# Clustered attention and mixture of experts: the sum of values as one more column of the values' products

## The chip, the cores and the metric

The kernel runs on one core of one Trainium2 chip. The metric is the device time of one execution in microseconds (us), from the start of the program on the core to its end. The core has five engines that work through queues of their own: PE (TensorE, matrix products; PEld is its loading of weights), DVE (VectorE), ACT (ScalarE), POOL (GpSimd) and SP (SyncE, which issues the transfers). Each queue is worked off in order, so an instruction that waits holds up all that stand behind it on its engine.

## The reference

An attention over clusters feeds a mixture of eight experts. Shortened:

```
q, k, v: (B=4, H=8, S=768, D=64); centroids: (8, 16, 64)
mask   = cluster(q)[..., :, None] == cluster(k)[..., None, :]     # cluster: argmax over 16 centroids
scores = where(mask, q @ k.T / 8, -1e9);  scores -= scores.max(-1)
attn   = exp(scores);  attn /= attn.sum(-1) + 1e-9
x      = attn @ v                                                # to (3072, 512)
P      = exp(x @ w_gate - max), then 8 rounds of normalizing over experts and over rows
out    = sum over e of P[:, e] * (relu(x @ w1[e]) @ w2[e])       # w1: (8, 512, 1024), w2: (8, 1024, 512)
```

A query whose cluster holds no key of its head has only masked scores. They are all equal, so its row is the mean of the head's values. This is the case of a "query without a key" that the change is about.

## The kernel before, in words

The program has two stages. The first is the attention, at 0 to about 490 us; the second is the experts, from about 487 us on, with a short overlap.

**Attention.** The 32 heads (4 batches of 8) are worked as 16 pairs. For one pair the 768 queries are cut into 512 and 256 columns and the 768 keys into six tiles of 128; CHUNKS holds nine pieces for each head, of which six are one key tile by 512 queries and three are two key tiles by 256 queries. For each head the stages are these:

- `max_chunk` (L845, L849): products for the row maxima, and a reduction on DVE.
- `max_rows` (from L857): the six maxima of a query become one, split into two half-precision rows that the scores' product subtracts. It also writes `flags` (L871), one where a query has no key, and makes `mz` (L894, ACT), the same mark as a row, which two transfers for each head put into `nht` (L908).
- `exp_chunk` (L926, L927, L933, L955): the scores' products, the exponential on ACT into a tile `pe`, and the sum of `pe` over key tiles, on POOL for all but the last pair, where DVE may do it. There are PB = 14 tiles `pe`.
- `values` (L991, L999): for one pair `av` collects `vn` (values, stationary) by `pe` (moving) over the six key tiles, in three blocks of eight products; each f32 product shows as two instructions. Two more products, `ve` by `nht` (L999), add the mean of the values where a query has no key. ACT then copies `av` to `xT` (L1011).
- `norm` (L1029 to L1113): the sums over keys, with 1e-9 and `flags` added (L1045), their reciprocal, spread over a tile `bc` by transfers, and the product with `xT` (L1086; for the last pair L1113).

`load_group` loads the values of four heads and makes their mean. For the first two of the eight groups it does so by twelve products with ones (L599), for the other six by two reductions on DVE (L607) and one product of two instructions (L611). Three small steps (L614, L618, L622) write it to `ve`. The pair's values can start once this is done.

**Experts.** Every product of the experts runs on PE in an order written out by hand (`run_pe`: L1600 and L1784); DVE, ACT and POOL prepare inputs and weights and gather outputs around it. The inputs of a batch are brought to a common scale by a power of two. For batches 0 to 2 this scale is found during the attention. For batch 3 `next_x` does it among the experts' products: it loads the batch (`xqB`), takes the largest value for each partition on DVE (L330, four reductions, and L1508), and finds the largest over partitions with `powers_spread`: a transfer to memory (L281), a transfer back that spreads all values to each partition (L284), a reduction on DVE (L288) and a few small steps (L290 to L313). Then ACT scales the inputs (L1516), they are split (L1526, L1528), stored (L1531) and loaded as `x6` (L1562).

There is a second way to the same scale, `powers` (L258): a PE transpose (L262), a reduction on DVE (L264), three small DVE steps (L266 to L269) and a small PE product (L272) that spreads the result. It is used in the attention.

**Order.** A planner writes the order of all instructions ahead of time. Each step names its engine, a planned duration and what it waits for; each has an urgency (KEYS); the planner then simulates the engines and fixes each engine's queue. Tokens stand for buffers (`t_pe` for `pe`, `t_x` for PSUM tiles, `t_nh` for `nht`). On the chip the order of each queue stays as planned, whatever the real durations are.

Of the kernel before, what the change touches and what calls it, by code (L numbers as in the profile page):

```python
# [8 lines left out]
F32 = mybir.dt.float32  # L9
# [15 lines left out]
P = 128  # L25
# [154 lines left out]
def attn_moe_kernel(  # L180
# [24 lines left out]
    PB = 14  # L205
# [17 lines left out]
    row = const.tile([2, 1], F32, name="row")  # L223
    nc.gpsimd.iota(row, pattern=[[0, 1]], base=0, channel_multiplier=1, allow_small_or_imprecise_dtypes=True)
    sgn = const.tile([2, 1], F32, name="sgn")
    nc.vector.tensor_scalar(out=sgn, in0=row, scalar1=-2.0, scalar2=1.0, op0=ALU.mult, op1=ALU.add)
    first = const.tile([2, 1], F32, name="first")
    nc.vector.tensor_scalar(out=first, in0=row, scalar1=-1.0, scalar2=1.0, op0=ALU.mult, op1=ALU.add)

# [127 lines left out]
    with ExitStack() as actx:  # L357
# [88 lines left out]
        flags = [sm.tile([P, 2 * NT], F32, name=f"flags{i}", bufs=1) for i in range(4)]  # L446
        row4 = sm.tile([4, 1], F32, name="row4", bufs=1)
        nc.gpsimd.iota(row4, pattern=[[0, 1]], base=0, channel_multiplier=1, allow_small_or_imprecise_dtypes=True)
        up2 = sm.tile([4, 1], F32, name="up2", bufs=1)
        nc.vector.tensor_scalar(out=up2, in0=row4, scalar1=2.0, scalar2=None, op0=ALU.is_ge)  # L450
        odd = sm.tile([4, 1], F32, name="odd", bufs=1)
        nc.vector.scalar_tensor_tensor(out=odd, in0=up2, scalar=-2.0, in1=row4, op0=ALU.mult, op1=ALU.add)
        sgn4 = sm.tile([4, 1], F32, name="sgn4", bufs=1)
        nc.vector.tensor_scalar(out=sgn4, in0=odd, scalar1=-2.0, scalar2=1.0, op0=ALU.mult, op1=ALU.add)
        halves = sm.tile([4, G, D], F32, name="halves", bufs=1)
        for x in range(2):
            c_ = sm.tile([4, 1], F32, name=f"of{x}", bufs=1)
            nc.vector.tensor_scalar(out=c_, in0=up2, scalar1=float(x), scalar2=1.0 / S, op0=ALU.is_equal, op1=ALU.mult)
            for g in range(x, G, 2):
                nc.vector.tensor_copy(halves[:, g], c_.broadcast_to([4, D]))  # L460
# [14 lines left out]
        minus = const.tile([P, 1], F32, name="minus")  # L475
        nc.vector.memset(minus, -1.0)
# [77 lines left out]
        t_nat, t_sc, t_pe, t_nh, t_vn = Tokens(2), Tokens(1), Tokens(PB), Tokens(6), Tokens(2)  # L554
        t_half = Tokens(2)
        t_sum = Tokens(4)
        t_mean, t_norm, t_row = Tokens(1), Tokens(2), Tokens(1)
# [18 lines left out]
        def load_group(n):  # L576
            b, g = n // H, n % H // G
            hs = slice(g * G, (g + 1) * G)
            if True:
                yield ev["x", 0, 1, "k"]  # L580
            if n >= G:
                yield ev["e", 0]
            yield t_vn
            t = groups[(b, g)] = {}
            yield SP, 0.625
            vn = vals.tile([P, G, NT, D], F32, name="vn")
            nc.sync.dma_start(
                out=vn.rearrange("p h t d -> p h (t d)"), in_=v[b, hs].rearrange("h (p t) d -> p h (t d)", t=NT)
            )
            yield plan.copied(3.2) - plan.now.time  # L590

            plan.now.key = urgency("vsum", n)
            yield t_mean
            if n < 2 * G:
                yield t_x
                yield PE, 1.3, 0.107, 0.12
                ps = misc_tile()
                for i in range(NT):
                    nc.tensor.matmul(ps[:, 0 : G * D], ones, vn[:, :, i, :], start=(i == 0), stop=(i == NT - 1))  # L599
            else:  # L600
                vsum = None
                for i in range(2):
                    yield DVE, 1.5
                    if i == 0:
                        vsum = nat.tile([P, G, D], F32, name="vsum", bufs=1)
                    hh = slice(i * G // 2, (i + 1) * G // 2)
                    nc.vector.tensor_reduce(out=vsum[:, hh], in_=vn[:, hh].rearrange("p h t d -> p h d t"), axis=AX, op=ALU.add)  # L607
                yield t_x
                yield PE, 0.64, 0.107, 0.213
                ps = misc_tile()  # L610
                nc.tensor.matmul(ps[:, 0 : G * D], ones, vsum.rearrange("p h d -> p (h d)"), start=True, stop=True)  # L611
            yield DVE, 0.4
            ms = sm.tile([4, G * D], F32, name="ms", bufs=1)
            nc.vector.tensor_tensor(out=ms, in0=ps[0:4, 0 : G * D], in1=halves.rearrange("p h d -> p (h d)"), op=ALU.mult)  # L614
            t_x.put(plan)
            yield ACT, 0.45
            mh = sm.tile([4, G * D], F32R, name="mh", bufs=1)
            nc.scalar.activation(mh, ms, AF.Copy, scale=sgn4)  # L618
            yield ev["cleared"]
            yield "DVE*", 0.4  # L620
            ve = ves[n // G % 2]
            nc.vector.scalar_tensor_tensor(  # L622
                out=ve[0:4].rearrange("p h d -> p (h d)"), in0=ms, scalar=odd, in1=mh.bitcast(F32), op0=ALU.mult, op1=ALU.add
            )
            t_mean.put(plan)
            t.update(vn=vn, ve=ve)
            ev["group", b, g].set(plan)
# [227 lines left out]
        def max_rows(n):  # L855
# [4 lines left out]
            if n >= 8:  # L860
                yield ev["norm", n // 2 - 4]
            yield t_x
            yield DVE, 0.6
# [3 lines left out]
            o = n % 2 * NT  # L867
# [3 lines left out]
            nc.vector.tensor_scalar(out=flags[n // 2 % 4][:, o : o + NT], in0=mr, scalar1=-BIG / 2, scalar2=None, op0=ALU.is_le)  # L871
            ev["flags", n].set(plan)
            half = ps.bitcast(F16)
            if n < 2:
# [5 lines left out]
                nc.tensor.transpose(out=half[0 : 2 * NT, P : 2 * P], in_=two.rearrange("p j t -> p (j t)"), identity=ident_h)  # L880
# [11 lines left out]
            yield ACT, 0.3  # L892
            mz = sm.tile([NT, P], F32R, name="mz")
            nc.scalar.activation(mz, half[0:NT, P : 2 * P], AF.Relu, scale=-4.0 * MARK / BIG, bias=minus[0:NT, :])  # L894
            t_x.put(plan)
            if n >= 2:
# [6 lines left out]
            yield t_nh  # L903
            yield ev["cleared"]
            yield SP, 1.25
            nh = nhs[n // 2 % 3]
            for j in range(n % 2 * 2, n % 2 * 2 + 2):
                nc.sync.dma_start(out=nh[j : j + 1, :].bitcast(F32).rearrange("o (t p) -> o t p", p=P), in_=mz.bitcast(F32))  # L908
            ev["nh", n].set(plan, plan.copied(0.2))

        def exp_chunk(n, c):
# [47 lines left out]
        def release(p, c):  # L959

            c2 = c + 1 if c == 0 else c
            for x in range(2):
                yield ev["s", 2 * p + x, c2]
                t_pe.put(plan)

        def values(p):
# [10 lines left out]
            ve = gr["ve"][:, h % G : h % G + 2].rearrange("p h d -> p (h d)")  # L977
            nh = nhs[p % 3]
            av = None
            for u in range(NCH // VU):  # L980
# [14 lines left out]
            for x in range(2):  # L995
                yield ev["nh", n + x]
            yield PE, 0.44, 0.107, 0.11
            for a, z in SPANS:
                nc.tensor.matmul(av[:, a:z], ve, nh[:, a:z], start=False, stop=True, skip_group_check=True)  # L999
            if h % G == G - 2:  # L1000
                t_vn.put(plan)
            for x in range(2):
                t_nh.put(plan)
                ev["v", n + x].set(plan)
            if h == 0:
                if b:
                    yield ev["batch", b - 1]
                xts[b] = sm.tile([P, NC, S], F32, name="xT", bufs=1)
            for a, z in SPANS:
                yield ACT, 0.15 + (z - a) * 0.00083  # L1010
                nc.scalar.copy(xts[b][:, h // 2, a:z], av[:, a:z])  # L1011
# [5 lines left out]
        def norm(p):  # L1017
# [23 lines left out]
            for x in range(2):  # L1041
                yield ev["flags", n + x]
            yield DVE, 0.2
            rs = work.tile([P, R], F32, name="rs")
            nc.vector.scalar_tensor_tensor(  # L1045
                out=rs.rearrange("p (g j) -> p g j", g=4),
                in0=ps2[:, 0 : NT // 2 * P].rearrange("p (j g q) -> p g j q", g=4, q=Q)[:, :, :, 0],
                scalar=1e-9,
                in1=flags[p % 4].rearrange("p (g j) -> p g j", g=4),
                op0=ALU.add,  # L1050
                op1=ALU.add,
# [5 lines left out]
            if p < npairs - 1:  # L1057
# [24 lines left out]
                x_ = xts[b][:, h // 2, :]  # L1082
# [828 lines left out]
```

## Time and profile before

| | |
|---|---|
| time, median of 3 runs | 2285.37 us (2284.19 to 2285.90) |
| time of the profiled execution | 2290.8 us |
| its span, first to last instruction | 2289.0 us |
| PE busy | 2207.9 us, 96% |
| DVE busy | 1877.2 us, 82% |
| ACT busy | 1201.2 us, 52% |
| POOL busy | 1375.3 us, 60% |
| mean granted TensorE clock | 0.989 |

The profiled execution is one run of its own, 5.4 us above the median; 1.8 us of it lie outside the span. Busy shares are averages over both stages. The stage of the experts takes about 1,800 us, so that the shares of the page are mostly its shares.

### The profile page before, as it was taken

The page shows a single profiled execution, that of the slowest core. Times are in us where ns is not written, and L with a number is a line of the kernel's source. Part 1 is how long each engine was busy: PE and PEld are TensorE (multiplying, and loading weights), DVE is VectorE, ACT ScalarE, POOL GpSimd, SP SyncE. Part 2 cuts the span into 40 slices and gives each one's busy share as a digit, 9 for nine tenths or more (in the row PEclk, how much of TensorE's full clock was granted, in tenths as well). Part 3 has the DMA queues.
Part 4 walks back from the last instruction along what each step waited for, and adds up shares of the span by engine and source line. Part 5 has one row for each costly group of instructions (what it writes and reads, how often), then busy time and mean ns, then how long its engine had stood idle before and what let it go on. Part 6 is the DMA issues. An engine that isn't in the chain of part 4 may idle for free.

```text
span 2289.0 us, 43195 instructions
## 1 busy us (share of the span) xinstructions
PE 2207.9 (96%) x16246; PEld 1530.3 (67%) x16246; DVE 1877.2 (82%) x3684; ACT 1201.2 (52%) x2325; POOL 1375.3 (60%) x1328
## 2 busy tenths in 40 slices
PE   5999999988989999999999999999999999999998
PEld 2444444436757777777777777777777777777777
DVE  7889888869977997788779877987797789777776
ACT  6776766756545545454535454545454444445432
POOL 4677777978645757464737373747465655546432
PEclk8999999999999999999999999999999999999999
DMA  3566552434421534162425232533444253414242
GB/s 94 134 141 171 131 133 78 172 132 142 160 101 63 180 87 143 59 195 78 140 72 185 70 116 86 171 85 101 126 134 119 65 170 89 134 49 137 59 139 77
DMA packets 172779, 270.03 MB, mean 118 GB/s; under 512 B 56100, under 2 KB 105368, under 8 KB 172056
## 3 DMA queue, kind: packets, MB, share of 16 engines
q1 hardware_dynamic: 172568, 267.26, 39.3%
q8 instruction: 127, 2.08, 0.4%
q14 instruction: 84, 0.69, 0.1%
HBM read 225.82 MB, written 23.69 MB: 109 GB/s over the span
## 4 chain that ended last, share of the span: by engine, by line
PE 85%; DVE 9%; ACT 2%; issue 1%; POOL 1%; DMA 1%; SPq 0%; DVEq 0%; ACTq 0%; POOLq 0%
PE a_ps L1600 21%; PE a_ps L1784 14%; PE ac_ps L1784 12%; PE c_ps L1784 11%; PE c_ps L1600 10%; PE b_ps L1600 5%; PE av_ps L991 4%; DVE mrt L849 2%; PE max_ps L845 2%; PE exp_ps L926 2%; PE exp_ps L927 1%; POOL psum L955 1%; ACT pe L933 1%; DVE c L1714 0%; DVE q L679 0%
## 5 line engine op out<-in xcount | busy, mean ns | idle before, releaser
L1784 PEld LDWEIGHTS <-h 128*128 128x128 f16 x8064 | 789.9, 98 | 192.2 <-issue 7.5
L1600 PEld LDWEIGHTS <-wa 128*128 128x128 f16 x5376 | 526.6, 98 | 279.0 <-issue 18.5
L1640 POOL TENSOR_TENSOR h<-s,h 128x384 f16<-128x384 f32 x127 | 124.8, 982 | 541.1 <-ACT h L1638 532.5
L1629 ACT ACTIVATE h<-c 128x384 f16<-128x384 f32 x384 | 201.2, 524 | 438.7 <-DVE c L1623 437.3
L1784 PE MATMUL a_ps<-wb,h 128*128 128x256 f16 x3072 | 377.2, 273 | 0.6 <-DVE acc L1824 0.6
L1784 PE MATMUL ac_ps<-wb,h 128*128 128x256 f16 x2688 | 367.8, 273 | 1.1 <-DVE acc L1820 1.1
L1824 DVE SCALAR_TENSOR_TENSOR acc<-a_ps,gates,acc 128x256 f32<-128x256 f32 x460 | 215.2, 479 | 88.6 <-PE a_ps L1784 85.8
L955 POOL TENSOR_TENSOR psum<-psum,pe 128x256 f32<-128x256 f32 (+1 forms) x240 | 256.5, 1098 | 51.9 <-ACT pe L933 49.5
L1784 PE MATMUL c_ps<-wb,h 128*128 128x256 f16 x2304 | 283.3, 273 | 3.5 <-DVE acc L1820 2.3
L1640 POOL TENSOR_TENSOR h<-c,h 128x384 f16<-128x384 f32 x252 | 248.5, 998 | 27.8 <-ACT h L1638 26.5
L1631 DVE SCALAR_TENSOR_TENSOR h<-c,h 128x384 f16<-128x384 f32 x384 | 256.1, 670 | 7.3 <-ACT h L1629 7.0
L933 ACT ACTIVATE pe<-exp_ps,escs 128x512 f32<-128x512 f32 x288 | 190.2, 685 | 58.0 <-PE exp_ps L927 52.7
L1824 DVE SCALAR_TENSOR_TENSOR acc<-ac_ps,gates,acc 128x256 f32<-128x256 f32 x402 | 192.4, 479 | 34.4 <-PE ac_ps L1784 32.0
L1824 DVE SCALAR_TENSOR_TENSOR acc<-c_ps,gates,acc 128x256 f32<-128x256 f32 x344 | 155.8, 477 | 75.2 <-PE c_ps L1784 74.7
L849 DVE TENSOR_REDUCE mrt<-max_ps 128x1 f32<-128x512 f32 (+1 forms) x288 | 188.8, 682 | 30.7 <-PE max_ps L845 27.3
L1620 ACT ACTIVATE c<-a_ps 128x384 f32<-128x384 f32 x256 | 125.3, 489 | 162.3 <-PE a_ps L1600 161.3
L1638 ACT CAST h<-c 128x384 f16<-128x384 f32 x256 | 128.3, 510 | 80.2 <-DVE c L1714 79.9
L1640 POOL TENSOR_TENSOR h<-h,h 128x384 f16<-128x384 f32 x124 | 141.5, 1141 | 36.0 <-PE c_ps L1784 23.9
L991 PE MATMUL av_ps<-pe,vn 128*64 128x512 f32 (+1 forms) x768 | 134.7, 494 | 0.0
L926 PE MATMUL exp_ps<-T 128*128 128x512 f16 (+1 forms) x384 | 121.8, 330 | 11.7 <-ACT pe L933 9.2
L845 PE MATMUL max_ps<-X 96*128 96x256 f16 (+1 forms) x384 | 107.5, 336 | 16.2 <-DVE mrt L849 11.4
L1620 ACT ACTIVATE h<-a_ps 128x384 f32<-128x384 f32 x128 | 62.9, 491 | 113.2 <-PE a_ps L1600 113.0
(495 smaller groups left out, 3759.6 us busy)
## 6 DMA issues: line engine op xcount, KB each, us to landing
raw<-in_moe_w SPq DMA_DIRECT2D x120, 512.0 KB
qn<-in_q SPq DMA_DIRECT2D x16, 384.0 KB
kn<-in_k SPq DMA_DIRECT2D x16, 384.0 KB
vn<-in_v SPq DMA_DIRECT2D x8, 768.0 KB
xd<-xT SPq DMA_DIRECT2D x4, 1536.0 KB
xqB<-xd SPq DMA_DIRECT2D x16, 384.0 KB
out<-acc SPq DMA_DIRECT2D x16, 384.0 KB
X<-T SPq DMA_DIRECT2D x60, 96.0 KB
```

The costliest lines, as they stand in the source:

```text
L849: nc.vector.tensor_reduce(out=t["mr"][:, i0 : i0 + ni, ni - 1], in_=ps.rearrange("p (x c) -> p x c", x=ni), axis=AX, op=ALU.max)
L926: nc.tensor.matmul(o, t["k1"][:, ki], t["q1"][:, a:z], start=True, stop=False)
L933: nc.scalar.activation(pe, ps.rearrange("p (x c) -> p x c", x=ni), AF.Exp, scale=pairs[p]["exp"])
L955: (nc.gpsimd if w == POOL else nc.vector).tensor_tensor(out=st[:, a:z], in0=old[a], in1=part, op=ALU.add)
L991: nc.tensor.matmul(av[o, a:z], vn[:, i, :], heads[t]["pe", c][:, i - i0], start=(i == 0), stop=False, skip_group_check=True)
L1600: nc.tensor.matmul(ps[:, 0:HB], wt[:, w_, a, c, :], xv[:, x_, c, :], start=(n in (0, 1, 5) and s_ == 0), stop=(s_ == len(steps) - 1), skip ...
L1620: nc.scalar.activation(t, ps[:, 0:HB], func, scale=KAPPA)
L1629: nc.scalar.activation(t[:, 0], c, AF.Relu)
L1631: nc.vector.scalar_tensor_tensor(out=t[:, 1], in0=c, scalar=0.0, in1=t[:, 0], op0=ALU.max, op1=ALU.subtract)
L1640: by(w).tensor_tensor(out=t[:, 1], in0=c, in1=t[:, 0], op=ALU.subtract)
L1784: nc.tensor.matmul(view(m, i), t[:, a_, i * P : (i + 1) * P], w[:, b_, x, :], start=(opens and n == 0 and i in (0, 2)), stop=(n == 5), ski ...
L1824: nc.vector.scalar_tensor_tensor(out=to, in0=src, scalar=gate[b, e][:, ti : ti + 1], in1=to, op0=ALU.mult, op1=ALU.add)
```

## The change

The mean for queries without a key is no longer made by itself. Each of the six `pe` tiles of two key tiles by 256 queries gets a 257th column that holds 2^-60 and is written once at the start (`pend`). The values' product over 257 columns then yields, in a 769th column of `av`, 2^-60 times the sum of the head's values. ACT copies it along to `xT`, which is one column wider, and the product with `bc` adds it before it multiplies: (x + column) / (sum + 768 * 2^-60). For a query without a key this is the mean; for all others the added term is too small to count.

So `nht`, `ve`, `flags`, `mz`, the two products L999, the means in `load_group` and the constants for them go. `pe` becomes two pools, 12 tiles of one kind and 6 of the other. L1086 becomes a `scalar_tensor_tensor` that DVE alone does (it had been open to POOL in the planner; all 15 ran on DVE). And in `next_x` the scale of batch 3 is found by `powers` on the PSUM tile that the gates use (`g_tile`), not by `powers_spread`.

```diff
-    PB = 14
+    PB = {1: 12, 2: 6}
+    FEW = 2.0**-60
...
-        nhs = [sm.tile([P, S], F32R, name=f"nht{i}", bufs=1) for i in range(3)]
-        ves = [sm.tile([P, G, D], F32R, name=f"ve{i}", bufs=1) for i in range(2)]
...
+        ends = [work.tile([P, 2, S - N0 + 1], F32, name=f"pend{i}", bufs=1) for i in range(PB[2])]
+        for t in ends:
+            nc.gpsimd.memset(t[:, :, S - N0 : S - N0 + 1], FEW)
...
 (load_group)
-            plan.now.key = urgency("vsum", n)
-            yield t_mean
-            if n < 2 * G:
-                yield t_x
-                yield PE, 1.3, 0.107, 0.12
-                ps = misc_tile()
-                for i in range(NT):
-                    nc.tensor.matmul(ps[:, 0 : G * D], ones, vn[:, :, i, :], start=(i == 0), stop=(i == NT - 1))
-            else:
...
-            t.update(vn=vn, ve=ve)
-            ev["group", b, g].set(plan)
+            t.update(vn=vn)
+            ev["group", b, g].set(plan, plan.copied(3.2))
...
 (max_rows)
-            nc.vector.tensor_scalar(out=flags[n // 2 % 4][:, o : o + NT], in0=mr, scalar1=-BIG / 2, scalar2=None, op0=ALU.is_le)
...
-                yield ev["nh", n - 2]
...
-            mz = sm.tile([NT, P], F32R, name="mz")
-            nc.scalar.activation(mz, half[0:NT, P : 2 * P], AF.Relu, scale=-4.0 * MARK / BIG, bias=minus[0:NT, :])
...
-                nc.sync.dma_start(out=nh[j : j + 1, :].bitcast(F32).rearrange("o (t p) -> o t p", p=P), in_=mz.bitcast(F32))
...
 (exp_chunk)
-            yield t_pe
+            yield t_pe[ni]
             yield ACT, 0.6
-            pe = t["pe", c] = work.tile([P, ni, z - a], F32, name="pe", bufs=PB)
+            if ni == 1:
+                full = work.tile([P, 1, N0], F32, name="pe", bufs=PB[1])
+            else:
+                full = ends.pop(0)
+            t["pe", c] = full
+            pe = full[:, :, 0 : z - a]
...
 (values)
-                                av[o, a:z], vn[:, i, :], heads[t]["pe", c][:, i - i0], start=(i == 0), stop=False, skip_group_check=True
+                                av[o, a : z + ni - 1], vn[:, i, :], heads[t]["pe", c][:, i - i0], start=(i == 0), stop=(i == NT - 1), skip_group_check=True
...
-            for x in range(2):
-                yield ev["nh", n + x]
-            yield PE, 0.44, 0.107, 0.11
-            for a, z in SPANS:
-                nc.tensor.matmul(av[:, a:z], ve, nh[:, a:z], start=False, stop=True, skip_group_check=True)
...
-                xts[b] = sm.tile([P, NC, S], F32, name="xT", bufs=1)
+                xts[b] = sm.tile([P, NC, S + 1], F32, name="xT", bufs=1)
...
 (norm)
-                if (yield ("DVE*", 0.88), (POOL, 1.75, RELUCT[9])) == POOL:
-                    nc.gpsimd.tensor_tensor(out=x_, in0=bc, in1=x_, op=ALU.mult)
-                else:
-                    nc.vector.tensor_tensor(out=x_, in0=bc, in1=x_, op=ALU.mult)
+                yield "DVE*", 0.88
+                nc.vector.scalar_tensor_tensor(out=x_, in0=x_, scalar=xts[b][:, h // 2, S : S + 1], in1=bc, op0=ALU.add, op1=ALU.mult)
...
 (next_x)
-            yield t_raw
-            yield from input_scale(b, am, raw_tile(), gs, powers_spread)
-            t_raw.put(plan)
+            yield t_g
+            yield ROOM
+            yield from input_scale(b, am, g_tile, gs)
+            t_g.put(plan)
```

## Rows read from the trace of the kernel before

**Rows 1.** Stretches: busy us (instructions) of PE, PEld, DVE, ACT, POOL; clock; DMA share, GB/s.

```profile
300.00:350.00 50.00, 48.25 (x333) 24.16 (x332) 41.93 (x100) 30.91 (x57) 37.55 (x37) 1.00 0.49 119
600.00:700.00 100.00, 88.64 (x652) 64.17 (x650) 79.67 (x164) 52.95 (x109) 47.73 (x42) 0.97 0.38 130
700.00:1000.00 300.00, 300.00 (x2302) 225.02 (x2300) 249.06 (x476) 152.41 (x301) 180.31 (x174) 1.00 0.36 109
```

**Rows 2.** Order of time on PE, 304 to 310 us: start, duration, instruction.

```profile
304.66 2.80 PE L991 MATMUL av_ps<-pe,vn 128*64 128x512 f32 x16
...
307.39 0.61 PE L999 MATMUL av_ps<-nht,ve 128*128 128x512 f32 x2
307.85 0.39 PE L926 MATMUL exp_ps<-T 128*128 128x512 f16 x1
308.08 0.38 PE L927 MATMUL exp_ps<-X 98*128 98x512 f16 x1
...
309.17 0.59 PE L611 MATMUL misc_ps<-vsum,ones 128*128 128x256 f32 x2
309.61 0.38 PE L926 MATMUL exp_ps<-T 128*128 128x512 f16 x1
```

**Rows 3.** The chain that ended last, 0 to 150 us: start, duration, what.

```profile
35.97 5.13 PE misc_ps L599 x12
...
79.69 2.59 PE misc_ps L599 x12
...
123.36 6.92 DMA vn<-in_v
```

**Rows 4.** The chain that ended last, 616 to 640 us.

```profile
616.78 3.45 DVE am L330 x4
...
620.44 8.28 DMA largest<-am
...
628.78 4.98 DMA raw<-largest
...
635.75 2.08 PE a_ps L1600 x6
...
638.97 0.97 PE a_ps L1600 x6
```

**Rows 5.** Waits of PE, 600 to 700 us: total us, times, longest.

```profile
PE a_ps L1600 <- DMA x6T<-xsd3T: 3.6, 1, 3.6
PE a_ps L1600 <- DVE c L1623: 2.8, 1, 2.8
PE c_ps L1600 <- ACT c L1620: 2.2, 1, 2.2
```

**Rows 6.** Order of time on DVE at 634 us: idle before and its releaser in brackets.

```profile
633.79 0.29 DVE L288 TENSOR_REDUCE gm<-raw 128x1 f32<-128x128 f32 x1 [3.97 <-DMA raw<-largest]
```

**Rows 7.** Instructions by line, 0 to 540 us: busy, mean ns, idle before, releaser.

```profile
L607 DVE TENSOR_REDUCE vsum<-vn 128x128 f32<-128x768 f32 x12 | 17.8, 1494 | 2.1 <-DMA vn<-in_v 2.1
```

**Rows 8.** One line's instructions: duration in ns (least/median/most), first and last start.

```profile
L991 PE MATMUL av_ps<-pe,vn x768: 379/486/1116, 65.6 to 485.6; 128*64 128x512 f32 x96, 128*64 128x256 f32 x96
...
L1086 DVE TENSOR_TENSOR xT<-bc,xT x15: 935/1085/2035, 102.6 to 485.4; 128x768 f32<-128x768 f32 x15
...
L1714 DVE SCALAR_TENSOR_TENSOR s<-c,h x128: 544/550/2270, 504.8 to 2265.4; 128x384 f32<-128x384 f32 x128
```

**Rows 9.** Order of time on PE: the two products of the scale, two instances.

```profile
311.48 0.27 PE L262 MATMUL misc_ps<-ident,amx 128*1 128x128 f32 x1
...
313.19 0.38 PE L272 MATMUL misc_ps<-gd,ones 1*128 1x1 f32 x2
...
330.87 0.27 PE L262 MATMUL misc_ps<-ident,am 128*2 128x128 f32 x1
...
336.43 0.38 PE L272 MATMUL misc_ps<-gd,ones 2*128 2x2 f32 x2
```

**Rows 10.** The page's costliest groups: the sums over keys on POOL.

```profile
L955 POOL TENSOR_TENSOR psum<-psum,pe 128x256 f32<-128x256 f32 (+1 forms) x240 | 256.5, 1098 | 51.9 <-ACT pe L933 49.5
```

More of the change, by code (lines that the diff above doesn't have):

```diff
@@ L222, in attn_moe_kernel @@
     nc.gpsimd.iota(rev, pattern=[[-1, C]], base=C, channel_multiplier=0, allow_small_or_imprecise_dtypes=True)
[L223 to L228, printed above, removed]
     lg = resid.tile([P, NTT, E], F32, name="lg")
@@ L553, in attn_moe_kernel @@
         t_x, t_s, t_m, t_v = Tokens(2, LIFT), Tokens(2), Tokens(2), Tokens(1)
[L554 removed]
+        t_nat, t_sc, t_pe, t_vn = Tokens(2), Tokens(1), {k: Tokens(n) for k, n in PB.items()}, Tokens(2)
         t_half = Tokens(2)
         t_sum = Tokens(4)
[L557 removed]
+        t_norm, t_row = Tokens(2), Tokens(1)
         pairs = {}
@@ L589, in load_group @@
             )
-            yield plan.copied(3.2) - plan.now.time
-            plan.now.key = urgency("vsum", n)
-            yield t_mean
-            if n < 2 * G:
-                yield t_x
-                yield PE, 1.3, 0.107, 0.12
-                ps = misc_tile()
-                for i in range(NT):
-                    nc.tensor.matmul(ps[:, 0 : G * D], ones, vn[:, :, i, :], start=(i == 0), stop=(i == NT - 1))
-            else:
[L601 to L625, printed above, removed]
-            t.update(vn=vn, ve=ve)
-            ev["group", b, g].set(plan)
+            t.update(vn=vn)
+            ev["group", b, g].set(plan, plan.copied(3.2))
         def wait_buffers(p):
@@ L859, in max_rows @@
             qa = t["qa"]
-            if n >= 8:
-                yield ev["norm", n // 2 - 4]
             yield t_x
-            yield DVE, 0.6
+            yield DVE, 0.5
             ps = misc_tile()
@@ L879, in max_rows @@
                     nc.tensor.transpose(out=av[0:2, i * P : (i + 1) * P], in_=two[:, :, i], identity=ident_h)
-                nc.tensor.transpose(out=half[0 : 2 * NT, P : 2 * P], in_=two.rearrange("p j t -> p (j t)"), identity=ident_h)
+                t_x.put(plan)
                 yield ACT, 0.8
@@ L891, in max_rows @@
                 nc.scalar.copy(mt, half[0 : 2 * NT, P : 2 * P])
-            yield ACT, 0.3
-            mz = sm.tile([NT, P], F32R, name="mz")
-            nc.scalar.activation(mz, half[0:NT, P : 2 * P], AF.Relu, scale=-4.0 * MARK / BIG, bias=minus[0:NT, :])
-            t_x.put(plan)
-            if n >= 2:
+                t_x.put(plan)
                 for j in range(2):
@@ L963, in release @@
                 yield ev["s", 2 * p + x, c2]
-                t_pe.put(plan)
+                ni = CHUNKS[c][1]
+                if ni == 2:
+                    ends.append(heads[2 * p + x]["pe", c])
+                t_pe[ni].put(plan)
         def values(p):
@@ L1040, in norm @@
                 nc.tensor.transpose(out=ps2[:, j * P : (j + 1) * P], in_=sc[:, j * P : (j + 1) * P], identity=ident)
-            for x in range(2):
-                yield ev["flags", n + x]
-            yield DVE, 0.2
+            yield DVE, 0.1
             rs = work.tile([P, R], F32, name="rs")
-            nc.vector.scalar_tensor_tensor(
+            nc.vector.tensor_scalar(
                 out=rs.rearrange("p (g j) -> p g j", g=4),
                 in0=ps2[:, 0 : NT // 2 * P].rearrange("p (j g q) -> p g j q", g=4, q=Q)[:, :, :, 0],
-                scalar=1e-9,
-                in1=flags[p % 4].rearrange("p (g j) -> p g j", g=4),
+                scalar1=S * FEW,
+                scalar2=None,
                 op0=ALU.add,
-                op1=ALU.add,
             )
@@ L1112, in norm @@
                     x_ = xts[b][:, h // 2, a:z]
-                    nc.vector.tensor_tensor(out=x_, in0=ps[:, 0 : z - a], in1=x_, op=ALU.mult)
+                    nc.vector.scalar_tensor_tensor(
+                        out=x_, in0=x_, scalar=xts[b][:, h // 2, S : S + 1], in1=ps[:, 0 : z - a], op0=ALU.add, op1=ALU.mult
+                    )
                     t_x.put(plan)
@@ L1118, in norm @@
                     amxs[b] = sm.tile([P, NC], F32, name="amx4")
-                largest(amxs[b][:, h // 2 : h // 2 + 1], xts[b][:, h // 2])
+                largest(amxs[b][:, h // 2 : h // 2 + 1], xts[b][:, h // 2, 0:S])
             ev["normed", p].set(plan)
@@ L1128, in out_batch @@
             yield SP, 0.625
-            nc.sync.dma_start(out=xd[b], in_=xts[b])
+            nc.sync.dma_start(out=xd[b], in_=xts[b][:, :, 0:S])
             ev["stored", b].set(plan, plan.copied(4.4))
@@ L1188, in scan_first @@
             t_x.put(plan)
-        def clear():
-            yield ev["x", 0, 1, "k"]
-            for t in nhs + ves:
-                yield POOL, 0.75 if t in nhs else 0.3
-                nc.gpsimd.memset(t.bitcast(F32), 0.0)
-            ev["cleared"].set(plan)
-        plan.spawn(clear(), urgency("rows", 0))
         for p in range(npairs):
```

31 lines of the change are left out of this document (2 added, 29 removed).

## The prediction

> **What bounds the kernel now.** I read the busy time by stretches first. In the attention PE is busy 48.25 of 50 us and DVE 41.93; among the experts PE is busy all of the 300 us from 700 on, but only 88.64 of the 100 us from 600 on [rows 1]. So there are three places to look at: the steady attention, its start, and the stretch at 600 to 700.
>
> In the attention, a busy PE need not be a full one, so the order of time on PE comes next: a product of 512 columns is shown with 0.38 to 0.39 us, but the next starts 0.23 us behind it, and the block of values' products is followed at once by the next product [rows 2]. The queue is full by its starts too, not only by its busy time. The chain of waits agrees for most of the stretch: it runs over PE, with stretches on DVE between. Its rows that belong to this change are the means' twelve products of the first two groups, and a wait of DVE for the values' transfer [rows 3].
>
> The Trainium skill (Trace Analysis, section "Identifying the Most-Contended Engine") says that matmul busy time is no good measure of how full TensorE is, and that the loading of weights should be read instead. By that rule PE, whose loading of weights takes 24.16 of 50 us [rows 1], has room to spare and its terms below would be nothing. The starts speak against it in this stretch; the case stands among the rivals.
>
> At 600 to 700 PE does 652 instructions, against 2302 / 3 = 767 for 100 us of the undisturbed stretch [rows 1]: 115 missing, at 7.67 for each us 15 us. The chain there shows four reductions on DVE, then a transfer of 8.28 us, another of 4.98, then a block of six products in 2.08 us, of which a later one takes 0.97 [rows 4]; the waits of PE are 3.6, 2.8 and 2.2 us [rows 5]. One DVE instruction (L288) waits for the second transfer, with DVE idle for 3.97 us [rows 6]; behind it in DVE's queue stand the experts' steps L1631 and L1623, for which PE waits 2.8 us, and ACT's scaling of the inputs, which ends in the late `x6`, the 3.6 us.
>
> **The change part by part.**
>
> *Products that go.* L999: from its start to that of the next product 307.85 - 307.39 = 0.46 us [rows 2]; 16 pairs make 7.4 us. L611: 309.61 - 309.17 = 0.44 us [rows 2], in six groups 2.6 us. L599 of the second group: 2.59 us on the chain, and of the first 5.13 us [rows 3], the same twelve products at twice the length, so at half clock. I take 3 of these 5.1 us, since at the start DVE and ACT still have to produce what PE would do instead. Sum 7.4 + 2.6 + 2.6 + 3 = 15.6 us. From it I take the last three L999, 1.4 us, since near the end POOL's sums and ACT's exponentials set the pace: 14.2 us.
>
> *DVE's steps that go.* The reductions L607 take 17.8 us [rows 7]. DVE has slack in the steady stretch, so they count only where PE then waited. Once, DVE stands 2.1 us idle for the values [rows 7]; the transfer is on the chain from 123.36 to 130.28 [rows 3], and the reduction of 1.49 us [rows 7] follows. PE waits behind it. I take 2.5 us, with 0 as the lower end and 6.9 + 1.5 = 8.4 us, the two rows of the chain, as the upper. Flags, `mz`, their small steps and 64 transfers' issues on SP lie beside PE's work: counted at nothing. Were PE not the bound, DVE's part would be all that is gained there.
>
> *What is added.* 257 for 256 columns: a block of eight logical products takes 307.39 - 304.66 = 2.73 us [rows 2] for 2 heads x 1536 columns, two heads at a time by that length, so 1.8 ns a column; four extra columns in a block, by twos, make 4 ns, in 48 blocks 0.2 us. L991's two forms are of 512 and 256 columns [rows 8]; no row shows an f32 product of an odd count. So the bounds are 0.2 us and the price of the dear column below; I take 0.2, as the block's length fits its columns. L1086: the old form takes at least 935 ns for 768 elements, the new kind 544 ns for 384 [rows 8], so between the same 935 and 2 x 544 = 1088 ns; the bound above is 16 x 0.15 = 2.4 us of DVE, which has lost 17.8 us, so nothing. The six memsets of one column go out before the planner's steps, beside the start. ACT's copies grow by one column of 257. The 18 tiles `pe` instead of 14 can only loosen a wait.
>
> *A wait that moves.* The values no longer wait for `ve` and `nht`, only for the load `vn`; behind it on PE stands everything else. The load of a later group is issued long before its use (at 123 us for heads that come into `values` after 150), so 6.9 us of transfer stay hidden.
>
> Attention: 14.2 + 2.5, say 17 us; lower end 6 (half of the steady PE terms, nothing else), upper 24 (all of 15.6 and all of 8.4).
>
> *Scale of batch 3.* 8.28 + 4.98 = 13.3 us of transfers [rows 4] go. In their place come a transpose, four DVE steps and a product. In the attention these take from 313.19 + 0.38 - 311.48 = 2.1 us to 336.43 + 0.38 - 330.87 = 5.9 us, depending on what DVE does between [rows 9]. The scale is ready 7 to 11 us earlier and nothing waits in DVE's queue for memory. But PE, whose order is fixed, now waits itself if DVE is late with the largest values or with the small steps; everything of the experts is queued behind it. The four reductions of 3.45 us stay [rows 4]. Of the 8.6 us of waits [rows 5] I expect nearly all to go, and of the 2.08 us block, which at 0.97 would run at full clock, about 1; with less PE waiting `x6` is needed earlier, so that some of the 3.6 us may stay, but other lost products in the 15 us come back. I take 9 us; ends 0 and 14.
>
> The Trainium skill (DMA: Bandwidth & Descriptors, "Latency and other measured facts") puts the fixed cost of a transfer at about 2 us, so two at about 4 us, as an estimate by that page. By it the new way would be no shorter than the old, and this term 0. The trace has 8.28 and 4.98 us for these two, and it decides.
>
> *Sum.* 17 + 9 = 26 us. The profiled execution took 2290.8 us, span 2289.0, so it would be 2265. The median before is 5.4 us lower, 2285.4: 2285.4 - 26 = 2259.4; I say 2260.
>
> **The rivals.**
>
> *Attention set by other work.* If DVE and POOL carry it, the PE terms vanish. POOL's sums take 256.5 / 240 = 1.07 us each [rows 10], 20 for each pair, 21.4 us, against (485.6 - 65.6) / 16 = 26.3 us for a pair [rows 8]. So POOL has room for 4.9 us a pair, more than the 1 us that goes. Left would be 2.5 + 9 us and little else: about 2273. Chance 0.14. The rule of the Trainium skill's Trace Analysis on matmul busy time, cited above, would end here too.
>
> *The wait for the scale is replaced by another.* PE stands for DVE's steps, or `x6` stays late because DVE's reductions and splits set it: gain 17 + 0 to 2, about 2267. For it: DVE is near full there (79.67 of 100 us [rows 1]), against it: 4 us of that it was idle in front of L288 [rows 6]. Chance 0.13. The figure of the Trainium skill's DMA page, cited above, would end here too.
>
> *Both.* The attention gives 2 to 4 us and the scale nothing: 2282, within the bound below. Chance 0.08.
>
> *The 257th column is dear.* If an f32 product with an odd count, or one from a tile that starts at 1028 bytes, went at half rate, the 256-column third of each block would double: 2.73 / 3 = 0.91 us, in 48 blocks 44 us, and 2260 becomes 2304, slower than before. It decides from 26 / 48 = 0.54 us a block on, that is when these products take 1.6 times as long. For it nothing in the trace; against it only that time follows columns there. Chance 0.08.
>
> **How the numbers follow.** Forecast, both parts at least half as large as taken: 0.57. Attention set elsewhere 0.14, scale's wait replaced 0.13, both 0.08, dear column 0.08. A measurement of this kernel tells about 0.2%, 4.6 us, from no change. Faster: 0.57 + 0.14 + 0.13 = 0.84; same 0.08; slower 0.08. Low end: 24 + 14 = 38 us gained, 2247. High end: 6 us gained, 2279; this takes in the first two rivals and leaves out the last two, 0.16.
>
> **What the profile after would show.** L599, L611, L999, L607 are gone, and the blocks of L991 still follow each other at 2.73 us; a longer block means the dear column. The last values' product ends near 469 instead of 486 us. At 600 to 700 no DVE instruction waits for a transfer, and PE does over 715 of its 767 instructions. The prediction is wrong if PE in the attention shows new waits for DVE or ACT as long as the products removed, if the pair period stays at 26 us, or if PE waits 2 us and more at the scale's transpose.

## The result, and the profile after

The changed kernel takes 2260.02 us (median of four runs, 2258.53 to 2262.31), against 2285.64 us (2284.19 to 2287.03) for the kernel before beside it: 0.9891 of the time, with an interval of 0.9877 to 0.9905. That is 25.6 us less; 26 were forecast.

The execution profiled after took 2258.53 us, 1.5 below its median; the one before lay 5.4 above. So the two traces differ by 32 us where the medians differ by 25.6, and a difference of a few us between two traces is no finding by itself. The page's head and its busy time by engine:

```profile
span 2256.8 us, 42824 instructions
...
PE 2187.1 (97%) x16179; PEld 1518.8 (67%) x16179; DVE 1849.7 (82%) x3612; ACT 1190.8 (53%) x2285; POOL 1362.5 (60%) x1328
```

The same stretches as in [rows 1], after:

```profile
300.00:350.00 50.00, 50.00 (x346) 24.32 (x345) 37.37 (x69) 30.90 (x58) 38.77 (x39) 1.00 0.45 103
600.00:700.00 100.00, 99.93 (x766) 74.76 (x765) 83.36 (x170) 60.89 (x125) 57.93 (x47) 1.00 0.27 93
700.00:1000.00 300.00, 300.00 (x2300) 224.82 (x2299) 253.79 (x476) 149.51 (x293) 187.08 (x182) 1.00 0.42 128
```

In the attention PE is busy all of the 50 us, and DVE 37.37 us where it had 41.93. From 600 to 700 us PE does 766 instructions, which is the 767 of the undisturbed stretch; before it did 652. From 700 us on PE is busy without a gap in both.

Where the time came from is seen when the start of the same block of PE's work is read in both traces (us; the last column is after less before):

| block | before | after | difference |
|---|---|---|---|
| first product for row maxima | 25.5 | 25.2 | -0.3 |
| first exponential's product | 43.6 | 37.5 | -6.0 |
| 97th | 170.3 | 160.2 | -10.1 |
| 241st | 331.1 | 310.5 | -20.6 |
| 361st | 458.9 | 435.7 | -23.2 |
| first of the experts | 487.2 | 465.1 | -22.1 |
| experts, instruction 733 | 612.2 | 590.9 | -21.3 |
| instruction 787 | 619.6 | 602.0 | -17.6 |
| instruction 949 | 649.1 | 623.5 | -25.6 |
| instruction 1327, and all later ones | 705.0 | 672.7 | -32.2 |

There are two gains: about 21 us come in the attention, 6 of them before its first exponential, and about 11 around the scale of batch 3. At the end of the attention the difference shrinks a little, and at the scale it first shrinks by 4. A second trace of the changed kernel (taken with the experiments) has each of these blocks 0.5 to 1.0 us later than the first; that much is a trace's own.

The values' products, one line's instructions by form (least, median and most ns, first and last start):

```profile
L921 PE MATMUL av_ps<-pe,vn x384: 591/592/932, 58.8 to 463.0; 128*64 128x512 f32 x192
...
L921 PE MATMUL av_ps<-pend,vn x384: 377/380/383, 60.6 to 464.1; 128*64 128x257 f32 x192
```

The first starts 6.8 us earlier and the last 21.5 us earlier than in [rows 8], so 14.7 us were gained between. The 257 columns cost nothing that shows: on the chain of waits a block of sixteen of these products takes 2.74 us, where the block before took 2.73 ([rows 2], from its start to the next product's).

```profile
311.86 2.74 PE av_ps L921 x16
```

The waits of PE around the scale, 550 to 610 us, and PE's order of time there (start, duration, idle before in brackets):

```profile
PE b_ps L1515 <- DMA x4B<-xsd2B: 1.7, 1, 1.7
PE g_ps L256 <- DVE am L1422: 1.6, 1, 1.6
PE c_ps L1699 <- DVE acc L1735: 1.2, 1, 1.2
```

```profile
595.77 1.14 PE L1515 MATMUL b_ps<-x4B,wa 128*128 128x384 f16 x6 [1.74 <-DMA x4B<-xsd2B]
...
599.17 0.27 PE L256 MATMUL g_ps<-ident,am 128*1 128x128 f32 x1 [1.61 <-DVE am L1422]
...
600.41 0.38 PE L266 MATMUL g_ps<-gd,ones 1*128 1x1 f32 x2
```

DVE's order of time in the same stretch:

```profile
595.41 3.52 DVE L324 TENSOR_REDUCE am<-xqB 128x1 f32<-128x768 f32 x4
598.96 0.16 DVE L1422 TENSOR_REDUCE am<-am 128x1 f32<-128x4 f32 x1
...
599.50 0.27 DVE L258 TENSOR_REDUCE gm<-g_ps 1x1 f32<-1x128 f32 x1
...
601.32 0.17 DVE L307 RECIPROCAL sx<-xinv 128x1 f32<-128x1 f32 x1
```

From the four reductions' end, 598.93 us, to the finished scale at 601.49 it takes 2.6 us; before, from 620.23 [rows 4] to the first instruction behind the second transfer at 633.79 [rows 6], 13.6 us went by, and the scale was not finished yet. No DVE instruction waits for memory there. In its place PE waits 1.6 us for the largest values, and 1.7 us for an input of the experts: its queue now gets there earlier than the data. With the two products of the scale themselves (0.27 and 0.38 us) these are the 4 us that the table shows lost before the gain. None of the waits of [rows 5] is left.

### The profile page after: what moved, and what is told of

Same layout as the page of the kernel before. It is cut to its first block, busy times and chain, and to the rows that moved or that the text cites. A ratio compares the mean times of both kernels' runs of the same rounds, so it can differ in the third digit from the quotient of the medians.

```text
span 2256.8 us, 42824 instructions
## 1 busy us (share of the span) xinstructions
PE 2187.1 (97%) x16179; PEld 1518.8 (67%) x16179; DVE 1849.7 (82%) x3612; ACT 1190.8 (53%) x2285; POOL 1362.5 (60%) x1328
## 4 chain that ended last, share of the span: by engine, by line
PE 87%; DVE 7%; POOL 2%; ACT 2%; issue 1%; DMA 0%; SPq 0%; DVEq 0%; POOLq 0%; ACTq 0%
PE a_ps L1515 21%; PE a_ps L1699 14%; PE ac_ps L1699 12%; PE c_ps L1699 11%; PE c_ps L1515 11%; PE b_ps L1515 5%; PE av_ps L921 4%; DVE mrt L790 2%; PE max_ps L786 2%; PE exp_ps L850 2%; PE exp_ps L851 2%; POOL psum L884 1%; PE misc_ps L691 1%; PE misc_ps L954 1%; DVE h L1546 1%
## 5 line engine op out<-in xcount | busy, mean ns | idle before, releaser
L884 POOL TENSOR_TENSOR psum<-psum,pe 128x512 f32<-128x512 f32 x120 | 156.7, 1325 | 33.0 <-ACT pe L862 30.4
L862 ACT ACTIVATE pe<-exp_ps,escs 128x512 f32<-128x512 f32 x192 | 128.6, 684 | 51.0 <-PE exp_ps L851 45.7
L851 PE MATMUL exp_ps<-X 98*128 98x512 f16 (+1 forms) x384 | 122.1, 331 | 0.3 <-ACT X L818 0.3
```

What stands on the lines that cost most here:

```text
L851: nc.tensor.matmul(o, t["k2"][0:98, ki], t["qa"][0:98, a:z], start=False, stop=True)
L884: (nc.gpsimd if w == POOL else nc.vector).tensor_tensor(out=st[:, a:z], in0=old[a], in1=part, op=ALU.add)
```

## The experiments

**Theory.** The attention is faster because PE, which sets its pace, has fewer products, and a little because DVE has fewer reductions; the rest comes from the scale, which no longer goes through memory. **Rivals.** DVE or POOL sets the attention, so that the reductions, or only the start, carry the gain; the scale's part exists only in a disturbed trace; or the new order of the queues, which a planner writes anew for each change, is worth as much as the instructions. Medians are given in us, with the ratio to the kernel before on the same chip. The kernel before had medians of 2285.6 to 2286.9 on the four chips, so medians of different chips compare to a little over 1 us. The changed kernel, taken again beside some of the experiments, had 2260.24 (0.9887, 0.9874 to 0.9901).

> The changed kernel, unchanged, on the same chip as the others of this call: 2258 to 2262 us, and a second profile that shows how much of a profile's time is its own.

### The two parts, each alone

The column without the new scale:

```diff
-            yield t_g
-            yield ROOM
-            yield from input_scale(b, am, g_tile, gs)
-            t_g.put(plan)
+            yield t_raw
+            yield from input_scale(b, am, raw_tile(), gs, powers_spread)
+            t_raw.put(plan)
```

> The changed kernel, but with batch 3's scale found by the two transfers as before. Theory (two separate gains, attention 17 and scale 9 us): 2265 to 2269 us. Rival (most of the gain is the scale's): 2275 us or more. Rival (the scale's wait comes back smaller, as the experts reach it in another state): 2262 us or less.

The scale without the column is the same edit the other way round, in the kernel before.

> The kernel before, with only batch 3's scale by products. Theory: the waits of 2.8, 2.2 and 3.6 us behind the second transfer go, one of 1 to 2 us on DVE's largest values comes: 9 us faster, 2275 to 2278 us, and 600 to 700 us holds over 715 PE instructions. Rival (replaced by another wait): 2282 us or more.

The column alone took 2269.26 (0.9921, 0.9907 to 0.9934), the scale alone 2281.15 (0.9971, 0.9962 to 0.9981). By the ratios, 0.79% and 0.29% make 1.08%, and both together gave 1.09%: the parts add up. The column is worth about 18 us and the scale 6.6 (4.3 to 8.7) when it comes alone. When it comes second it is worth about 7 by the ratios (0.9921 to 0.9891) and 9 by the medians of two chips (2269.26 to 2260.02). The column alone came out as expected; the scale alone lies between the 2275 to 2278 us expected and the rival's 2282. The stretch 600 to 700 us in the trace of the column alone, and then of the scale alone:

```profile
600.00:700.00 100.00, 91.18 (x669) 66.42 (x668) 74.40 (x157) 56.34 (x118) 50.73 (x43) 0.97 0.27 94
```

```profile
600.00:700.00 100.00, 96.57 (x726) 71.56 (x725) 84.09 (x177) 62.58 (x129) 54.96 (x47) 0.98 0.36 122
```

With the old scale PE is still at 669 instructions; with the new one at 726. The loss is not one trace's: from instruction 733 of the experts to instruction 1327 (the table above) PE takes 92.8, 90.9 and 92.0 us in the three traces with the old scale (the kernel before, the same with other planned durations, the column alone), and 81.8 to 84.8 us in the eleven with the new one (81.8 in both of the changed kernel, 83.4 with the scale alone). The two transfers took 7.91 and 4.66 us, and 7.69 and 4.65, in the second and third of these traces. So the rival that this part exists only in a disturbed trace falls. PE's wait in the trace of the scale alone, 590 to 680 us, is the one that the forecast named:

```profile
PE g_ps L262 <- DVE am L1508: 3.1, 1, 3.1
```

### Pairs' products back on PE

Two products per pair, of a tile of zeros, are added to the values' sum as L999 was; once with their duration known to the planner, and once without it, so that every queue keeps its order and they only take PE's time (the traces show the changed kernel's order of products with the 32 instructions put in).

```diff
+            yield PE, 0.44, 0.107, 0.11        (first kernel only)
+            for a, z in SPANS:
+                nc.tensor.matmul(av[:, a:z], ve0, nh0[:, a:z], start=False, stop=True, skip_group_check=True)
```

> The changed kernel with two products of zeros for each pair put back into the values' sum (128 by 512 and 128 by 256 columns, the shapes of the removed L999); nothing on DVE, ACT or SP comes back. Theory (PE's queue sets the attention): 16 x 0.46 = 7.4 us less 1.4 near the end, so 2265 to 2268 us. Rival (DVE sets it): at most 1 us, 2260 to 2261.

> As e3 (two products of zeros for each pair), but put in without telling the planner, so that every queue keeps the changed kernel's order. Theory (PE's queue sets the attention): 7.4 us less up to 1.4 near the end, 2265 to 2268 us, growing evenly from pair to pair. Rival (e3's 5 us came from its new order): 2260 to 2262 us.

Planned, they cost 5 us (2265.30; 0.9914, 0.99 to 0.9928). In the same order they cost 2.7 (2262.93; 0.9898, 0.9884 to 0.9913), which the ratios can't tell from nothing. That is below the 2265 to 2268 us expected and just above the rival's 2262. The trace of the latter shows where the rest of sixteen times 0.46 us goes. Against the changed kernel's trace it stands 2.2 us late at its first values' product, before any added product has run, 7.6 us at the 361st exponential's product, and 3.0 us at instruction 733 of the experts: about 5.4 us gather, and about 1 of them is left. Most of it is given back in the tail of the attention, which the last experiment here looks at. PE's granted clock there differs too: from 425 to 475 us its mean is 1.00 with the added products and 0.94 in the changed kernel (0.91 in that kernel's second trace). What of the give-back is POOL's and what the clock's was not told apart.

### DVE's reductions back

Twelve reductions of a group's values, as L607, whose result is not used; again planned, and in an unchanged order (there with a planned duration of 0).

```diff
+                for i in range(2):
+                    yield DVE, 1.5             (0.0 in the second kernel)
...
+                    nc.vector.tensor_reduce(out=vsum[:, hh], in_=vn[:, hh].rearrange("p h t d -> p h d t"), axis=AX, op=ALU.add)
```

> The changed kernel with the twelve DVE reductions over the values put back (their result is not used; the values of a group wait for them); no product comes back. Theory (DVE has slack, only the one wait for the transfer costs): 0 to 3 us, 2260 to 2263 us. Rival (DVE sets the attention): most of 12 x 1.49 = 17.8 us, 2270 us or more.

> As e4 (twelve reductions on DVE), but put in without telling the planner; every other instruction keeps the changed kernel's order, and no product waits for them. Theory (DVE has slack, the reductions delay what stands behind them now and then): 0 to 4 us longer than the changed kernel, and e4's gain was its order. Rival (the reductions cost nothing at all, e4's order apart): within 1 us. Rival (DVE sets the attention): 10 us or more longer.

This is the largest surprise. Planned, the kernel with 18 us more work on DVE is not slower but 3.7 us faster (2256.56; 0.9869, 0.9856 to 0.9883; the interval overlaps the changed kernel's, so that "not slower" is the safe part). None of its expectations had that. Put in without replanning, the same reductions cost 15.6 us (2275.88; 0.9951, 0.994 to 0.9963), nearly their whole time, as the last of the three expectations had it:

```profile
L577 DVE TENSOR_REDUCE vsum<-vn 128x128 f32<-128x768 f32 x12 | 17.5, 1477 | 0.0
```

PE's waits for the maxima, 100 to 450 us, rise to 13.1 us:

```profile
PE max_ps L795 <- DVE mrt L799: 13.1, 21, 2.9
```

In the kernel with the products in an unchanged order the same wait has

```profile
PE max_ps L791 <- DVE mrt L795: 7.1, 19, 1.5
```

and the changed kernel 7.7 us. In the planned version it is 7.1 too, and DVE's busy time from 100 to 450 us shows that the work is there, 300.26 us against 284.55 in the changed kernel (the planned version's row, then the changed kernel's):

```profile
100.00:450.00 350.00, 334.43 (x2157) 157.83 (x2153) 300.26 (x568) 236.24 (x420) 275.26 (x268) 1.00 0.50 133
```

```profile
100.00:450.00 350.00, 334.09 (x2150) 158.57 (x2146) 284.55 (x556) 237.08 (x420) 271.75 (x268) 0.99 0.51 134
```

So DVE has 15 us of room in these 350 us, but not where an order that was made without the reductions leaves them. Where they stand decides even within one run. In the unchanged order each of the six groups has two reductions, about 2.9 us of DVE. Against the changed kernel the exponentials' products fall behind in jumps, within 3 to 15 us after the start of five of these groups, by 3.4, 2.1, 4.8, 1.2 and 1.6 us; after the second group (at 175.1 and 180.6 us) they lose nothing. The largest jump falls where PE's granted clock is 0.93 (250 to 300 us; 1.00 in the changed kernel), which may be why it is more than the 2.9 us of work.

### The first groups' products back

Planned, the twelve products L599 of the two first groups with a copy of their result; in an unchanged order, two blocks of twelve products of 256 columns, of constants, in front of the transposes of the row maxima of heads 0 and 4.

```diff
+            for i in range(NT):
+                nc.tensor.matmul(ps[:, 256:512], ones, ident.unsqueeze(1).broadcast_to([P, 2, P]), start=(i == 0), stop=(i == NT - 1), skip_group_check=True)
```

> The changed kernel with the twelve products with ones put back for each of the first two groups (and one DVE copy of their result, which is not used). Theory (they stood in the way at the start: 2.6 us for the second group, 3 of the 5.1 us at half clock for the first): 5 to 6 us longer than the changed kernel. Rival (the start is set by DVE and ACT, and dense products end the half clock sooner): 0 to 2.6 us longer.

> Twelve products of the removed shape (128 by 256 columns, f32) put in at the row maxima of heads 0 and 4, about where the removed ones stood, on data that is there (ones and the unit matrix), without telling the planner. Theory (they stood in the way at the start): 3 to 5 us for the first, 2.6 for the second, 2265 to 2268 us. Rival (e5's 12 us were theirs): 2270 us or more. Rival (the start absorbs them): 2260 to 2262 us.

Planned they cost 12.5 us (2272.71; 0.9943, 0.993 to 0.9957), in an unchanged order 8.9 (2269.11; 0.9923, 0.9912 to 0.9935). PE's order of time in the latter shows both blocks (of the second, its ten last products):

```profile
37.74 5.49 PE L798 MATMUL misc_ps<-ident,ones 128*128 128x256 f32 x12 [1.97 <-DVE mr L812]
...
95.81 2.32 PE L798 MATMUL misc_ps<-ident,ones 128*128 128x256 f32 x10
```

Both lie outside what was expected: the planned one above 5 to 6 us, the other between 2268 and the rival's 2270. The first block takes 5.49 us, twice as long, as in [rows 3]; the clock granted in it was 0.50, that is 1.2 GHz. Against the changed kernel this one is 1 us late at its start, 5.4 at the first values' product, 8.0 at the 49th exponential's, and 8.9 at the experts. So the first block costs 4 to 5 us and the second 2.6, almost nothing of either is hidden, and the tail doesn't give it back: DVE's maxima, ACT's exponentials and POOL's sums are all late by the same time.

The first block stands here behind a wait of 1.97 us for DVE, so that nothing could lie under it; the removed one stood ahead of that wait. Whether it was hidden there can be read from the kernel before itself, since the trace with the scale alone has the same attention and ran that block at full clock (granted 1.00, 2.4 GHz, for 0.50 in the trace of the kernel before). The block and the first exponential's product, in the kernel before and then with the scale alone:

```profile
35.77 5.33 PE L599 MATMUL misc_ps<-vn,ones 128*128 128x256 f32 x12
...
43.59 0.38 PE L926 MATMUL exp_ps<-T 128*128 128x512 f16 x1
```

```profile
36.62 2.75 PE L599 MATMUL misc_ps<-vn,ones 128*128 128x256 f32 x12
...
41.88 0.38 PE L926 MATMUL exp_ps<-T 128*128 128x512 f16 x1
```

The block is 2.58 us shorter, and from its start to the first exponential it takes 5.26 us instead of 7.82: 2.56 us less. So its time passed on in full there as well. What its removal is worth depends on the clock of the execution.

### Nothing but the order

In the changed kernel two planned durations of steps that lost an instruction (0.5 and 0.1 us) get their values of before back. No instruction differs.

```diff
-            yield DVE, 0.5
+            yield DVE, 0.6
...
-            yield DVE, 0.1
+            yield DVE, 0.2
```

> The changed kernel with the two planned durations that it shortened (0.5 and 0.1 us) put back to 0.6 and 0.2 us; no instruction differs, only their order may. If an order of its own accounts for much of the result, the time moves by 3 us or more either way; if not, it stays within 1.5 us of the changed kernel.

The reverse in the kernel before:

> The kernel before with the changed kernel's two planned durations (0.5 for 0.6 and 0.1 for 0.2 us); no instruction differs, only the order. If the kernel before stood in a poor order, it gets faster by 3 us or more, 2282 us or less, and that much of the change's gain was luck of the order; if orders scatter evenly, it may as well get slower; within 1.5 us, and order matters little for it.

In the changed kernel this costs 5.1 us (2265.38; 0.9909, 0.9895 to 0.9922); in its trace 1625 of PE's 16179 products stand at another place. In the kernel before 1512 of 16246 do, and the time stays the same (2286.76; 1.0008, 0.9996 to 1.0021). So two orders of one program can differ by 5 us with no difference in work, and a replanned experiment (5.0 for the pairs' products, -3.7 for the reductions) measures its edit only to about that.

### The tail of the attention

The sums over keys of the last pair may go to DVE as well as POOL; here those of the last two pairs may.

```diff
-                if n < nheads - 2:
+                if n < nheads - 4:
```

> The changed kernel where the sums over keys of the last two pairs, not of the last one, may go to DVE. Theory (near the end POOL's sums set the pace, so that the last removed products bring nothing): PE's wait of 2.4 us for POOL goes and the stretch of 16 us on POOL shortens, 2 to 5 us shorter than the changed kernel. Rival (ACT and PE set the end too): within 1 us.

2254.50 us (2254.02 to 2256.73; 0.9865, 0.9851 to 0.9878): 5.7 us less than the changed kernel on the same chip, and so the fastest with the reductions' kernel above. The chain of waits of the changed kernel says what sets the time there (start, duration):

```profile
437.56 6.58 POOL psum L884 x6
```

PE's waits at 425 to 475 us begin with

```profile
PE misc_ps L954 <- POOL psum L884: 2.4, 1, 2.4
```

which the new kernel doesn't have. The stretch in the changed kernel, then in this one:

```profile
425.00:475.00 50.00, 39.70 (x213) 17.21 (x212) 26.10 (x40) 30.04 (x52) 31.69 (x28) 0.94 0.15 51
```

```profile
425.00:475.00 50.00, 42.35 (x248) 18.10 (x247) 39.09 (x66) 32.13 (x55) 16.21 (x14) 0.97 0.20 67
```

POOL goes from 31.69 to 16.21 us, DVE from 26.10 to 39.09, and PE does 248 instructions for 213. Against the changed kernel the start of the 361st exponential's product is 2.1 us later, that of the experts 2.4 us earlier. POOL's sums are therefore a bound at the end, and PE's work there has cover. This fits both findings on the products, though no run joins the two edits: slower pairs alone can let POOL keep its pace and lose little, while two blocks at the start delay POOL as well.

## Why the prediction was right, and where its steps were not

**The whole.** 26 us forecast, 25.6 measured; both parts are close as well: 17 for the attention against 18, and 9 for the scale against 6.6 alone and 7 to 9 as the second step. The likeliest case held. None of the signs of being wrong came in the changed kernel: from the first to the last start of the values' products a pair takes (464.1 - 58.8) / 16 = 25.3 us, not 26; PE's wait for the row maxima from 100 to 450 us is 7.7 us against 7.1 before; and PE waits 1.6 us at the scale's transpose.

**The scale** went as written. The transfers went, DVE's wait at the head of its queue with them, and 766 instructions are above the 715 asked for. PE waits for the largest values, as said: 1.6 us in the changed kernel, and 3.1 with the scale alone, which is above the 2 us named as a sign. The size, 9 us, was read from one trace; the same stretch in the other traces is 6 to 11 us shorter with the new scale, and the timed runs give 6.6 alone (4.3 to 8.7). So the term is right or somewhat too large.

The Trainium skill (DMA: Bandwidth & Descriptors, "Latency and other measured facts") puts the fixed cost of a transfer at about 2 us, by which the term would have been 0. The traces differ from it: the two transfers took 8.28 and 4.98 us [rows 4], and the gain of 0.29% decides against 0.

**The dear column** did not come: 2.74 us a block.

**The start** was mis-sized. 2.6 and 3 us were taken for L599. Put back in an unchanged order the two blocks cost 8.9 us; by the trace the second costs its 2.6 and the first 4 to 5. The step that failed is "I take 3 of these 5.1 us, since at the start DVE and ACT still have to produce what PE would do instead": PE's first exponential stood 6.0 us earlier, and in the kernel before a block that ran 2.58 us shorter brought the first exponential 2.56 us forward. So DVE and ACT hid next to nothing of it.

**The pairs' products** were priced right, but less of the price reaches the end. The step said 1.4 us of 7.4 lie under POOL; of the 5.4 us that gather in the trace about 1 stays, and 2.7 are timed. The reason given, POOL's pace near the end, is borne out by the last experiment, but its reach was taken too small; the clock may have a share.

**DVE's slack** was wrong as a general sentence. "DVE has slack in the steady stretch, so they count only where PE then waited" holds for an order that was made with the reductions in it (replanned they cost nothing, -3.7 us); set in blindly, they cost 15.6 of 17.5 us. The 2.5 us taken is between, and no single number is right: what a step on DVE costs depends on where it stands (from 0 to 4.8 us for the same two reductions) and on whether the order is made for it.

**A step that was missing** is the order itself. The new kernel gets a new order in all queues, and an order alone was worth 5.1 us in the changed kernel. The agreement of 17 and 18 us is therefore partly luck: the start was taken too small and the pairs' products too large, each by more than the sum is off.

**The rival that other work sets the attention** (2273) has fallen for the whole, but not everywhere: POOL sets the tail (5.7 us gained there), and DVE sets PE's pace in places. The Trainium skill (Trace Analysis, "Identifying the Most-Contended Engine") would judge how full TensorE is by the loading of weights, and by the share of the peak arithmetic, instead of by matmul busy time. By the loading alone this trace does not agree: from 300 to 350 us the changed kernel has 24.32 of 50 us of loading, while PE is busy for all 50 and has no wait listed.

**What stays open** is how the 18 us divide. In an unchanged order the pairs' products bring 2.7 and the first groups' 8.9; L611 was not put back at all, and the reductions only in orders that were not the kernel before's. Nor were the small steps on DVE that went with them, which the prediction counted at nothing: from 100 to 450 us of the kernel before, `flags` takes 4.0 us of DVE and `ve` 4.7, and PE waits 0.8 us for `flags`. The rest of about 6 us can't be told from the order.

## What to carry to other kernels

Put a removed step back twice, once with the queues planned anew and once with every queue in its old order: the first includes what a different order is worth (here 4 to 5 us either way), the second what the engine's time costs where it stands. A scale that goes through memory at the head of a queue that others share was worth replacing by a few products here (about 7 to 9 us), and its wait moved to the engine that now asks for the values. Where an engine is relieved, look at the tail of the stage first, since another engine may set it there: letting DVE take the sums of the last two pairs, not of the last alone, brought 5.7 us with one changed number.

## What the runs showed of the hardware

An f32 product of 257 columns costs what its columns cost: 380 ns shown, and 2.74 us for a block of sixteen instructions (2.73 with 256 columns), with an odd count and a tile that starts at 1028 bytes. Two small transfers, of 128 values to memory and back to all partitions, took 8.28 and 4.98 us to land [rows 4] with the DMA engines 0.38 busy [rows 1], and 7.7 to 7.9 and 4.7 us in two other traces. Twelve f32 products of 256 columns took 2.75 us at a granted clock of 1.00 (2.4 GHz) and 5.33 at 0.50 (1.2 GHz), at the same place in the same order of PE's work, in two executions.

Two traces of the same instructions stand apart by up to 1 us (the changed kernel twice), and by more where the clock differs: the trace with the new scale alone, whose attention is that of the kernel before, is 2.5 us ahead at the 49th product for row maxima and 2.8 at the experts, about as much as its twelve products at full clock saved. A time of one trace is not finer than that.
